# Loading v of two batches as fp32 through another queue, and turning x pair by pair, in a fused attention and squared-ReLU layer

## The chip, the cores and the metric

The kernel runs on one core of a Trainium2 chip. The metric is device time in microseconds (us), the median of the executions. The engines are TensorE (PE in the profile, PEld for its weight loads), VectorE (DVE), ScalarE (ACT), GpSimd (POOL) and SyncE (SP, which here issues transfers only). A line such as L1044 is line 1044 of the kernel before.

## The reference: what is computed

Attention with a relative bias over 8 batches of 8 heads, 576 positions and 64 dimensions, and then two dense layers with a squared ReLU between them:

```
B, H, S, D = q.shape                        # 8, 8, 576, 64, float32
scores = (1.0 / np.sqrt(D)) * np.matmul(q, k.transpose(0, 1, 3, 2))
scores = scores + bias.transpose(2, 0, 1)[None, :, :, :]   # bias_table[bucket(|i - j|)]
attn = np.exp(scores - max); attn = attn / (sum(attn) + 1e-09)
attn_out = np.matmul(attn, v)
x = attn_out.transpose(0, 2, 1, 3).reshape(B * S, H * D)   # 4608 x 512
h = np.maximum(x @ w_in, 0.0)               # w_in 512 x 2048
out = (h * h @ w_out)                       # w_out 2048 x 512, out float32
```

## The kernel before

The work on the chip is in fp16 with sums in fp32. A *pair* is two heads of one batch, so there are 32 pairs, four to a batch. A *group* is 512 rows of x, so there are nine; group 0 lies within batch 0. The program is laid out by a small planner at build time: each piece of work is added with the engines that may do it and their estimated durations, what it depends on, the buffers that it holds, a due time (its priority) and an earliest time; the planner then simulates all engines and writes the instructions in the order that it found. On the chip every engine runs its instructions in that order, each as soon as its data are there.

The constants that steer the plan (times in ns):

```
PERIOD, LEAD, FAST, FASTN = 9600.0, 1600.0, 3000, 7
AHEAD, G0, GP = 20600.0, 54700.0, 35900.0
RELU_DVE = 2
NSTG, NQK, NPT, NV, NX, NGB, NRT, NY = 5, 4, 3, 3, 6, 2, 4, 4
QUIET, LATER = 5200.0, 8500.0
TAB, EV = 6400.0, 1
ORDER = "k0 i0 q0 q1 v i1 i2 o0 k1 o1 i3 o2 o3"
...
def nominal(p):                       # when a pair is due
    return LEAD + FAST * min(p, FASTN) + PERIOD * max(p - FASTN, 0)
```

PSUM holds two score buffers of two banks, one bank for attention times v, and three banks (`g_ps`, ring `r_g`) for all else.

The first q and k come as fp32 into room of `g1` (a buffer that group 1 fills much later) and are cast. All other q, k, v and weights are loaded and cast to fp16 by transfers on GpSimd's queue. v of batch 0 goes head by head between the loads of q and k, v of batch 1 where ORDER has "v":

```
def load_v_head(b, h):
    l = load(
        "POOL", nc.gpsimd,
        lambda: vas[b_v[b].slot][:, :, h, 0:64],
        const(v[b, h, 0:512, :].rearrange("(t p) d -> p t d", p=128)),
        512 * 34.5, v_fix[min(b, 1)], [b_v[b]], pdue(),
    )
    ...
for hp in range(4):
    for w in range(2):
        if hp:
            load_six(hp, w)
        else:
            cast_first(w)
    if hp == 2:
        load_v_tail(0)
    if hp >= 1:
        for h in range(2 * hp - 2, 2 * hp):
            load_v_head(0, h)
for h in range(6, 8):
    load_v_head(0, h)
```

A few buffers have to be filled with constants once, by VectorE:

```
z_fix = [[fill(zz[:, 0], 0.0, 150.0, 10, QUIET)], [fill(zz[:, 1:], 0.0, 300.0, 11, LATER)]]
first = [fill(pt_sb[:, :, PW:], 1.0, 150.0, 20, LATER), fill(pm_sb[:, :, S:], 1.0, 150.0, 20, LATER)]
...   # v_fix: the same for the ones and zeros beside v
s_fix = [fill(stg[i][w][96:128, 512:640].bitcast(FP32), 0.0, 90.0, 40 + i, 25000.0) ...]
```

For the first three batches, q and k of a pair are turned by TensorE (L608) in twelve transposes each and evacuated by VectorE or ScalarE (L570, L572; pairs from 1 to EV-1 by VectorE alone):

```
if b < SIX:
    for j in range(6):
        for e in range(2):
            io(nc.tensor.transpose(ps[ds(64 * e, 64), ts(j, 96)], six(t)[:, e, ts(j, D)], id_sb[0:96, 0:96]))
```

A pair then goes on so: scores (L653, last queries L677, last keys L702), exponentials on ScalarE (L664, L687, L712), a multiply with the exponentials of the bias near the diagonal ("bands", VectorE, L745), attention times v with a column of sums (L781, L788), and a reciprocal and a multiply on VectorE (L805, L810), which leave x of the pair in SBUF. The bands need the bias tables, which TensorE builds (L353) and VectorE or ScalarE evacuates (L365, L367).

Layer 1 needs x turned. For batches 0 to 2 TensorE does this (L848) when all four pairs of the batch are through, one tile of 128 rows with four transposes at a time; for the later batches a transposing transfer does it:

```
def x_turn(b, norms):
    xb = [x_bufs[4 * b + hp] for hp in range(4)]
    for qt in range(5):
        bank = Buf(r_g)
        def tr(qt=qt, bank=bank):
            ps = g_ps[bank.slot].bitcast(FP16)
            for kk in range(4):
                io(nc.tensor.transpose(ps[:, ts(kk, 128)], xs[xb[kk].slot][:, qt, :], id_sb))
        ...
```

A tile of layer 1 is four matmuls over 512 columns (L1044), one for each pair of heads, as rows of x are 4 x 128 long. Its ReLU is done by ScalarE (L1065), or by either engine in groups below RELU_DVE (L1067), the square by VectorE (L1075). Layer 2 (L962) uses seven products of half matrices in place of eight.

```
def f1(nt=nt, bank=bank):
    ...
    for a, z, c in ((0, n, c), (n, GT, 0)):
        for kk in range(4 if z > a else 0):
            io(nc.tensor.matmul(g_ps[bank.slot][:, a:z], w_in_sb[:, kk, ts(nt, 128)],
                                xt_sb[:, kk, c : c + z - a], start=(kk == 0), stop=(kk == 3)))
...
o = P.add({"PE": 4 * mm(512)}, f1, xt_ready[g] + [l_win[nt // 4]], [bank, gb1], due + i * 2000, 0.0, "f")
```

Of the kernel before, what the change touches and what calls it, by code (L numbers as in the profile page):

```python
# [10 lines left out]
FP32 = mybir.dt.float32  # L11
# [19 lines left out]
PERIOD, LEAD, FAST, FASTN = 9600.0, 1600.0, 3000, 7  # L31
AHEAD, G0, GP = 20600.0, 54700.0, 35900.0
DT_X = 3
RELU_DVE = 2
NSTG, NQK, NPT, NV, NX, NGB, NRT, NY = 5, 4, 3, 3, 6, 2, 4, 4
QUIET, LATER = 5200.0, 8500.0
TAB, EV = 6400.0, 1
P_ORDER = "1 6 2 5 7 3 4"
P_LAST = "1 6 2 5 7 3 4"
SIX = 3  # L40
ORDER = "k0 i0 q0 q1 v i1 i2 o0 k1 o1 i3 o2 o3"
# [149 lines left out]
def kernel(  # L191
# [74 lines left out]
    def loader(eng_name, eng, out_, in_, packets, deps=(), bufs=(), due=0.0):  # L266
# [3 lines left out]
            {eng_name: 720.0 if eng_name == "POOL" else 600.0},  # L270
# [3 lines left out]
            due,  # L274
        )
# [10 lines left out]
    def load(eng_name, eng, out_, in_, packets, deps=(), bufs=(), due=0.0):  # L286
        return loader(eng_name, eng, out_, in_, packets, deps, bufs, due)[0]
# [15 lines left out]
        128 * 27, due=0,  # L303
# [21 lines left out]
        {"PE": 250.0},  # L325
# [21 lines left out]
    for c in range(6):  # L347
# [11 lines left out]
        o = P.add({"PE": 16 * 55.0}, t_mm, [o_eb, l_oh], [t_b], LEAD + TAB, 0.0, "f")  # L359
# [27 lines left out]
    def fill(ap, value, ns, due, after, deps=()):  # L387
# [3 lines left out]
    z_fix = [[fill(zz[:, 0], 0.0, 150.0, 10, QUIET)], [fill(zz[:, 1:], 0.0, 300.0, 11, LATER)]]  # L391
    first = [
        fill(pt_sb[:, :, PW:], 1.0, 150.0, 20, LATER),
        fill(pm_sb[:, :, S:], 1.0, 150.0, 20, LATER),
# [11 lines left out]
        fill(stg[i][w][96:128, 512:640].bitcast(FP32), 0.0, 90.0, 40 + i, 25000.0)  # L406
# [56 lines left out]
    def cast_first(w):  # L463

        def cast(o):
            src, dst = first_f[0:96, ts(w, 768)], stg[b_stg[0].slot][w][0:96, :]
# [6 lines left out]

    def load_v_head(b, h):
        l = load(
            "POOL", nc.gpsimd,
            lambda: vas[b_v[b].slot][:, :, h, 0:64],
            const(v[b, h, 0:512, :].rearrange("(t p) d -> p t d", p=128)),
            512 * 34.5, v_fix[min(b, 1)], [b_v[b]], pdue(),
        )  # L480
        l_v.setdefault((b, h // 2), []).append(l)
# [12 lines left out]
    def load_v(b):  # L494
# [9 lines left out]
        load_v_tail(b)  # L504

# [22 lines left out]
# [3 lines that stand above are left out]
                load_six(hp, w)  # L531
            else:
                cast_first(w)
        if hp == 2:
            load_v_tail(0)
        if hp >= 1:
            for h in range(2 * hp - 2, 2 * hp):
                load_v_head(0, h)
    for h in range(6, 8):
        load_v_head(0, h)  # L540
    for step in ORDER.split():
# [7 lines left out]
        else:  # L549
# [589 lines left out]
```

The softmax here doesn't subtract the row's maximum and nothing guards it: scores larger than these inputs give would overflow.

## Time and profile before

| | before |
|---|---|
| time, median of 3 | 377.01 us (376.7 to 378.59) |
| span of the profiled execution | 376.3 us |
| busy: TensorE, VectorE, ScalarE, GpSimd | 362.4, 269.0, 255.5, 178.3 us |
| transfers | 38.74 MB in 146,163 packets |
| software queue (GpSimd's) | 94,496 packets, 18.07 MB, 60.9% of the 16 engines |
| hardware queue (SyncE's) | 51,280 packets, 19.75 MB, 27.3% of the 16 engines |
| first matmul of L608 | 5.89 us |
| first matmul of layer 1 (L1044) | 41.24 us |

How to read it: the profile's page gives the busy time of each engine, the span cut into 40 slices with the busy share in tenths, the transfer queues, and the chain of work that ended last, followed back from the last instruction. A window gives the same busy times for one stretch. A busy TensorE isn't one at its peak, since matmuls overlap and their ends are modelled. Small groups of the page, in its columns (line, engine, operation, tiles, shapes and count; busy us and mean ns; idle time before them and what ended it), look so:

```profile
L271 POOL DMA_DIRECT2D va<-in_v_dram x36 | 30.8, 860 | 1.5 <-DMA qs<-in_q_dram 0.8
L635 POOL COPY qz<-kt 64x64 f16<-64x64 f16 x59 | 20.2, 342 | 33.3 <-DMA kt<-ks 17.4
```

The first is GpSimd issuing loads of v: 36 issues, 860 ns each. The second is a small copy on GpSimd.

### The profile page before, as it was taken

The numbers are of one execution on the slowest core, as the hardware profiler recorded it, in microseconds if no ns is written. First come the engines' busy times: TensorE is split into PE (matmuls) and PEld (weight loads), VectorE is DVE, ScalarE is ACT, GpSimd is POOL, SyncE is SP. The second block draws the span as 40 slices with busy tenths as digits, with TensorE's granted clock in tenths as the row PEclk, the third lists the DMA queues.
The fourth block names the chain that finished last, engine by engine and source line by source line (L and its number), as shares of the span: only waits on it lengthen the run. The fifth ranks groups of instructions, "written<-read, shape, count | busy, mean of one in ns | idle before, by whom it ended". The sixth has DMA issues, their size and how long they took to land.

```text
span 376.3 us, 10050 instructions
## 1 busy us (share of the span) xinstructions
PE 362.4 (96%) x4046; PEld 247.6 (66%) x4046; DVE 269.0 (71%) x612; ACT 255.5 (68%) x361; POOL 178.3 (47%) x318
## 2 busy tenths in 40 slices
PE   3988999999999999999999999999999999999996
PEld 2656555745778666687766765677577878556775
DVE  3987689998788677767685777757776683583653
ACT  4888979988557887866787778747885541564330
POOL 7876453889368583933758446583550000000000
PEclk9989999999999999999999999999999999999999
DMA  9999999699999999949999799999990222200103
GB/s 171 145 119 159 200 170 88 44 95 84 83 159 129 111 118 145 108 47 119 142 135 67 109 121 149 79 110 105 162 116 30 77 58 68 70 2 28 57 28 111
DMA packets 146163, 38.74 MB, mean 103 GB/s; under 512 B 128070, under 2 KB 146118, under 8 KB 146118
## 3 DMA queue, kind: packets, MB, share of 16 engines
q0 software_dynamic: 94496, 18.07, 60.9%
q1 hardware_dynamic: 51280, 19.75, 27.3%
q8 instruction: 31, 0.51, 0.6%
q10 hardware_dynamic: 342, 0.30, 0.3%
q14 instruction: 14, 0.11, 0.1%
HBM read 36.88 MB, written 9.44 MB: 123 GB/s over the span
## 4 chain that ended last, share of the span: by engine, by line
PE 90%; ACT 4%; DVE 3%; issue 1%; DMA 1%; ACTq 0%
PE f L1044 34%; PE f L962 29%; PE pv L788 10%; PE st L653 9%; PE pv L781 3%; PE st L702 2%; PE st L677 2%; ACT pt L664 1%; PE f L608 1%; DMA g<-in_k_dram 1%; ACT pt L687 1%; PE f L848 1%; DVE x L810 0%; ACT kt L570 0%; PE f L353 0%
## 5 line engine op out<-in xcount | busy, mean ns | idle before, releaser
L664 ACT ACTIVATE pt<-st 128x1024 f16<-128x1024 f32 x128 | 126.8, 1024 | 22.6 <-PE st L653 22.5
L1044 PE MATMUL f<-xt,w_in_sb 128*128 128x512 f16 (+4 forms) x704 | 142.1, 341 | 0.0
L1065 ACT ACTIVATE rt<-f 128x512 f16<-128x512 f32 x134 | 80.0, 598 | 62.0 <-PE f L1044 60.5
L1044 PEld LDWEIGHTS <-w_in_sb 128*128 128x128 f16 x704 | 62.6, 98 | 53.0 <-issue 10.8
L1075 DVE TENSOR_TENSOR g<-rt 128x512 f16<-128x512 f16 x144 | 60.7, 423 | 41.3 <-ACT rt L1065 40.2
L745 DVE TENSOR_TENSOR pt<-pt,tb_sb 128x1536 f16<-128x1536 f16 (+2 forms) x96 | 58.2, 621 | 10.6 <-ACT pt L664 10.2
L962 PEld LDWEIGHTS <-g 128*128 128x128 f16 x576 | 54.9, 98 | 15.4 <-issue 4.7
L788 PE MATMUL pv<-va,pt 128*128 128x65 f16 x1280 | 55.3, 194 | 0.0
L788 PEld LDWEIGHTS <-pt 128*128 128x128 f16 x1280 | 50.9, 98 | 2.9 <-issue 0.7
L271 POOL DMA_DIRECT2D qs<-in_q_dram x71 | 50.0, 725 | 2.4 <-DMA ks<-in_k_dram 1.1
L271 POOL DMA_DIRECT2D ks<-in_k_dram x71 | 50.0, 715 | 1.4 <-issue 1.4
L962 PEld LDWEIGHTS <-s 128*128 128x128 f16 x432 | 40.6, 98 | 10.6 <-issue 3.4
L635 POOL COPY qz<-qt 64x64 f16<-64x64 f16 x53 | 15.5, 293 | 64.2 <-DMA qt<-qs 35.5
L989 DVE SCALAR_TENSOR_TENSOR y<-f,y 128x512 f32<-128x512 f32 (+1 forms) x47 | 31.4, 667 | 16.1 <-PE f L962 15.1
L653 PE MATMUL st<-qt,kt 64*128 64x512 f16 x256 | 41.6, 396 | 1.1 <-ACT pt L664 0.5
L962 PE MATMUL f<-wt,g 128*128 128x256 f16 x288 | 36.6, 273 | 0.0
L962 PE MATMUL f<-w_out_sb,s 128*128 128x256 f16 x288 | 36.6, 273 | 0.0
L962 PE MATMUL f<-w_out_sb,g 128*128 128x256 f16 x288 | 36.2, 273 | 0.1
L781 PE MATMUL pv<-vm,pm 128*128 128x130 f16 x160 | 35.5, 222 | 0.5 <-DVE x L810 0.4
L635 POOL COPY qz<-kt 64x64 f16<-64x64 f16 x59 | 20.2, 342 | 33.3 <-DMA kt<-ks 17.4
L810 DVE TENSOR_TENSOR x<-pv,r 128x384 f16<-128x384 f32 x64 | 31.4, 490 | 1.9
L271 POOL DMA_DIRECT2D va<-in_v_dram x36 | 30.8, 860 | 1.5 <-DMA qs<-in_q_dram 0.8
(62 smaller groups left out, 308.0 us busy)
## 6 DMA issues: line engine op xcount, KB each, us to landing
out_dram<-y SPq DMA_DIRECT2D x34, 256.0 KB, 2.4
va<-in_v_dram POOLq DMA_DIRECT2D x28, 128.0 KB, 4.7
qs<-in_q_dram POOLq DMA_DIRECT2D x40, 64.0 KB, 3.2
ks<-in_k_dram POOLq DMA_DIRECT2D x40, 64.0 KB, 3.0
w_in_sb<-in_moe_w_in_dram POOLq DMA_DIRECT2D x4, 512.0 KB, 7.6
w_out_sb<-in_moe_w_out_dram POOLq DMA_DIRECT2D x4, 512.0 KB, 9.9
qs<-in_q_dram POOLq DMA_DIRECT2D x11, 144.0 KB, 5.0
ks<-in_k_dram POOLq DMA_DIRECT2D x11, 144.0 KB, 6.2
```

The source lines that it names most:

```text
L271: lambda: io(eng.dma_start(out=out_(), in_=in_())),
L635: io(eng.tensor_copy(out=dst[qb.slot][rw, rw], in_=src[qb.slot][rw, 512:576]))
L653: nc.tensor.matmul(sets_ps[st.slot][:, e, :], kt[rw, ts(jt, 128)], qt[rw, 0:512], start=True, stop=True,)
L664: nc.scalar.activation(out=p5(pts[pb.slot])[:, jt, :, 0:512], in_=sets_ps[st.slot], func=EXPF, scale=SCALE)
L745: io(nc.vector.tensor_tensor(out=a, in0=a, in1=t, op=MULT))
L781: nc.tensor.matmul(ps[:, i, :, :], pm[:, c : c + 128], vm[:, hp, :, 0:65], start=True, stop=False)
L788: nc.tensor.matmul(ps[:, i, e, :], pt[:, (2 * jt + e) * S + c : (2 * jt + e) * S + c + 128], va[:, jt, 2 * hp + e, 0:65], start=False, sto ...
L810: nc.vector.tensor_tensor(out=xs[xb.slot][:, qt0 : qt0 + nq, :].rearrange("p t (e d) -> p t e d", e=2), in0=ps[:, :, :, 0:64], in1=rs[rb.s ...
L962: nc.tensor.matmul(g_ps[bf.slot][:, ts(s_, HALF)], left(c, s_), right(c), start=(c == 0 and (s_ == 0 or apart) and i not in before), stop= ...
L1044: nc.tensor.matmul(g_ps[bank.slot][:, a:z], w_in_sb[:, kk, ts(nt, 128)], xt_sb[:, kk, c : c + z - a], start=(kk == 0), stop=(kk == 3),)
L1065: io(nc.scalar.activation(out=rts[rb.slot], in_=g_ps[bank.slot], func=RELUF))
L1075: nc.vector.tensor_tensor(out=gs[gb1.slot][:, nt, :], in0=rts[rb.slot], in1=rts[rb.slot], op=MULT)
```

## The change

It has three parts that can be seen in the data flow. v of batches 0 and 1 is fetched as fp32 through SyncE's queue into the upper part of `g1`, which group 1 needs only later, and cast by GpSimd into place; that takes these loads, with their cast, off GpSimd's queue. x is turned by pairs, not by batches, so that a pair's x is ready for layer 1 as soon as the pair is through. The first three tiles of layer 1 (PRE) are split: three of the four matmuls run when three pairs are there, the fourth when all are. Beside these, pair 0 is turned by six transposes of both heads at once, for which its cast lays the heads side by side; VectorE alone evacuates q and k of pairs 1 to 6 (EV); the constant fills come earlier (QUIET, LATER, FILL); the planner's estimates of several operations are set anew; the order of loads and the due times are others. The option PV_G is off.

The diff, cut to its core:

```
-PERIOD, LEAD, FAST, FASTN = 9600.0, 1600.0, 3000, 7
-AHEAD, G0, GP = 20600.0, 54700.0, 35900.0
+PERIOD, LEAD, FAST, FASTN = 8800.0, 2300.0, 3100.0, 8
+AHEAD, G0, GP = 22400.0, 56700.0, 44600.0
-RELU_DVE = 2
+RELU_DVE = 3
-QUIET, LATER = 5200.0, 8500.0
-TAB, EV = 6400.0, 1
-P_ORDER = "1 6 2 5 7 3 4"
+QUIET, LATER = 1500.0, 1500.0
+TAB, EV = 9000.0, 7
+P_ORDER = "1 2 6 5 7 3 4"
-ORDER = "k0 i0 q0 q1 v i1 i2 o0 k1 o1 i3 o2 o3"
+PV_G, PRE, FILL = 0, 3, 0
+V0_AT, V1_AT = 4600.0, 25300.0
+ORDER = "k0 i0 q0 k1 q1 i1 i2 i3 o0 o1 o2 o3"
...
-        o = P.add({"PE": 16 * 55.0}, t_mm, [o_eb, l_oh], [t_b], LEAD + TAB, 0.0, "f")
+        o = P.add({"PE": 16 * 33.0}, t_mm, [o_eb, l_oh], [t_b], LEAD + TAB, 0.0, "f")
...   (fills: 150 to 170 and 220, 300 to 380 ns)
-        fill(stg[i][w][96:128, 512:640].bitcast(FP32), 0.0, 90.0, 40 + i, 25000.0)
+        fill(stg[i][w][96:128, 512:640].bitcast(FP32), 0.0, 90.0, 40 + i, FILL)
...
+    room_f = gs[NGB - 1].bitcast(FP32).rearrange("p t c -> p (t c)")[:, 1536:]
+    def fetch_v(b):
+        rb = Buf(r_room)
+        for tt in range(4):
+            l = load("SP", nc.sync,
+                const(room_f[:, ts(tt, 512)].rearrange("p (h d) -> p h d", h=H)),
+                const(v[b, :, ts(tt, 128), :].transpose([1, 0, 2])),
+                1024 * 19, (), [rb], -0.5 + b, after=(V0_AT, V1_AT)[b])
+            o = P.add({"POOL": 780.0},
+                lambda tt=tt: io(nc.gpsimd.tensor_copy(
+                        out=vas[b_v[b].slot][:, tt, :, 0:64],
+                        in_=room_f[:, ts(tt, 512)].rearrange("p (h d) -> p h d", h=H))),
+                [l] + v_fix[min(b, 1)], [rb, b_v[b]], -1.0)
...   (the last 64 rows likewise: two loads and two casts of 420 ns)
-        if hp == 2:
-            load_v_tail(0)
-        if hp >= 1:
-            for h in range(2 * hp - 2, 2 * hp):
-                load_v_head(0, h)
-    for h in range(6, 8):
-        load_v_head(0, h)
+    for b in range(2):
+        fetch_v(b)
...
+                if p == 0:
+                    for j in range(6):
+                        io(nc.tensor.transpose(ps[:, ts(j, 96)], t[0:96, ts(j, 128)], id_sb[0:96, 0:96]))
...
-    def x_turn(b, norms):
+    def x_turn(p, norms):
+        b, hp = divmod(p, 4)
+        for part, qt0, nq in ((0, 0, 3), (1, 3, 2)):
+            bank = Buf(r_g)
+            n = min(128 * nq, S - 128 * qt0)
+            def tr(qt0=qt0, nq=nq, bank=bank):
+                ps = g_ps[bank.slot].bitcast(FP16)
+                for i in range(nq):
+                    io(nc.tensor.transpose(ps[:, ts(i, 128)], xs[xb.slot][:, qt0 + i, :], id_sb))
+            o = P.add({"PE": nq * mm(128)}, tr, [norms[part]], [bank, xb], T, 0.0, "f")
...   (one copy of 384 or 192 columns each, and xt_pair notes it)
+                ahead = 3 if g == 0 and i < PRE else 0
+                if ahead:
+                    o = P.add({"PE": ahead * mm(512)}, lambda f1=f1: f1(k1=3),
+                        [x for kk in range(ahead) for x in xt_pair[g, kk]] + [l_win[nt // 4]], [bank, gb1],
+                        due + i * 2000, 0.0, "f")
                 o = P.add(
-                    {"PE": 4 * mm(512)}, f1, xt_ready[g] + [l_win[nt // 4]], [bank, gb1], due + i * 2000, 0.0, "f"
+                    {"PE": (4 - ahead) * mm(512)}, lambda f1=f1, ahead=ahead: f1(k0=ahead),
+                    [o] + (v_cast if g == NGB - 1 else []) + xt_ready[g] + [l_win[nt // 4]], [bank, gb1], ...
```

## The prediction

> **What bounds the kernel now.** I read the page first, for who is busy, then the chain of waits, then windows of the first 80 us, then the timelines of the engines in the first 42 us. The page says TensorE (PE):
>
> ```profile
> PE 362.4 (96%) x4046; PEld 247.6 (66%) x4046; DVE 269.0 (71%) x612; ACT 255.5 (68%) x361; POOL 178.3 (47%) x318
> ...
> PEclk9989999999999999999999999999999999999999
> DMA  9999999699999999949999799999990222200103
> ...
> PE 90%; ACT 4%; DVE 3%; issue 1%; DMA 1%; ACTq 0%
> ```
>
> The Trainium skill ("Trainium Kernel Development and Optimization", Performance Expectations) warns that matmul busy time flatters, since matmuls overlap, and this trace agrees: the page's 96% hides gaps. So I add up what TensorE streams, with lengths read off the chain where it runs without a break: four layer-1 matmuls 0.86 us, 144 tiles: 124; eight layer-2 matmuls 0.87 us, 126 times: 110; a query tile of attention times v 0.06 + 0.24 us, 160 times: 48; four score matmuls 0.43 us, 64 times: 27.5; last keys 0.24 and last queries 0.22 us, 32 times each: 14.7; twelve transposes of q or k 0.315 us, 24 times: 7.6; x turned and bias tables about 6.5. Sum 338 us of a span of 376.3. The other 38 us: 5.9 before the first matmul, about 3 after the last, and 29 in gaps that busy time does not show. Layer 1 starts at 41.2 us. By then the trace has 40 score matmuls, 20 query tiles, 168 transposes of q and k, 96 table matmuls, 12 + 24 of the last keys and queries and 20 of x: 4.3 + 6.0 + 4.4 + 3.2 + 2.7 + 1.1 = 21.7 us of streaming in 35.3 us. So some 13.6 us are lost there and some 16 us in the 332 us after. The latter are mostly a fixed toll: a layer-1 tile after a change of the array's row mode takes 0.97 us instead of 0.86, and 54 groups of four scores lie after 41 us, each with a change in and out: 54 x 2 x 0.11 = 11.9 us. The change leaves those groups as they are. What can be won lies before 41 us.
>
> What limits that stretch is seen in the windows (columns: length, then busy us of PE, its weight loads, VectorE, ScalarE, GpSimd, granted clock, DMA share, GB/s):
>
> ```profile
> 14.00:18.00 4.00, 4.00 (x82) 2.67 (x78) 3.83 (x9) 3.50 (x5) 3.58 (x6) 1.00 1.72 111
> 18.00:22.00 4.00, 2.87 (x32) 1.52 (x33) 3.79 (x9) 3.79 (x6) 3.64 (x7) 0.84 1.11 147
> 22.00:26.00 4.00, 3.99 (x75) 3.00 (x73) 2.91 (x8) 3.21 (x6) 1.89 (x5) 0.73 1.78 137
> 26.00:30.00 4.00, 3.69 (x89) 2.95 (x89) 3.52 (x18) 4.00 (x6) 3.60 (x8) 1.00 0.89 58
> ```
>
> VectorE and ScalarE are both nearly full; TensorE waits for exponentials and for evacuated q and k. The clock dips there. The chain of waits in this stretch (start, length, what) shows whose work it is:
>
> ```profile
> 5.89 1.19 PE f L608 x24
> ...
> 8.97 0.38 DVE qz L388
> 9.35 0.21 DVE pt L388
> 9.56 0.21 DVE pm L388
> ...
> 9.83 0.50 DVE vm L388
> ...
> 10.63 0.77 DVE kt L572
> ...
> 24.80 1.03 ACT kt L570 x2
> 25.82 1.70 ACT pt L664 x2
> ...
> 40.32 0.45 PE f L848 x5
> 40.77 0.54 PE st L653 x4
> 41.31 2.70 PE f L1044 x12
> ```
>
> From 9 to 10.6 us the chain is nothing but memsets on VectorE (two short ones of 0.14 and 0.07 us follow those shown); at 24.8 it is ScalarE evacuating k ahead of exponentials. v is not on it: its eight head loads for batch 0 are issued from 7.5 to 16.6 us and land a median 4.7 us later, and the first attention times v, at 21.75 us, follows band multiplies on VectorE that begin at 20.28.
>
> **What the skill says.** "SBUF — State Buffer", SBUF: two separate sides: GpSimd and VectorE share one port pair, held for a whole instruction; it names VectorE operations in a two-port mode or with two SBUF inputs, and says that a GpSimd-queue DMA is held up when its descriptors can't be written. This trace is compatible: the same GpSimd copy of 64x64 takes 0.23 us alone, and four from 51.43 us took 2.47. "GPSIMD Engine Reference", Elementwise: a one-input loop at 1.8 cycles an element, 512 elements in 769 ns; no run here shows a fp32 cast on GpSimd yet. "DMA: Bandwidth & Descriptors", Why small descriptors are slow: a fixed overhead per packet, 27% for one of 256 B. The page of the profile agrees in kind: 94,496 software packets hold 60.9% of 16 engines, 376.3 x 16 x 0.609 / 94,496 = 38.8 ns each, though most are small.
>
> **The change, part by part.**
> 1. Memsets. Their earliest planned times go from 5.2 and 8.5 us to 1.5 us, where VectorE is idle (0.83 to 5.28 us), and the ten of the staging rows (26.20 to 26.97 us) to the start. On the chain this removes 0.38 + 0.21 + 0.21 + 0.50 + 0.14 + 0.07 = 1.5 us, and off it some 1.5 us of a nearly full VectorE. Gain 1.5 us.
> 2. Pair 0's q and k are turned by 6 transposes each instead of 12, as the cast lays both heads side by side: 24 took 1.19 us in the chain, 12 should take 0.6. Gain 0.6 us.
> 3. q and k of pairs 1 to 6 are evacuated by VectorE alone. ScalarE did 4 qt and 3 kt before 41.2 us (2.7 + 1.8 us), all but one of pairs after 0, so it loses about 3.9 us; VectorE gains six of 0.75, 4.5 us, less the 3.2 us of memsets taken away. The least work before batch 0 is through: ScalarE from 8.8 us, 4 pairs of 4 x 1.02 + 0.65 + 0.60 = 5.3 us, 21.3, and four or five further pieces of batch 1; VectorE from 5.9 us, tables 4.4, evacuations of pairs 0 to 5 about 8.3, bands 4 x (0.42 + 0.95 + 0.48 + 0.25) = 8.4, normalising 4 x (0.20 + 0.56 + 0.18 + 0.42) = 5.4, x 2.3, small copies 1.6: 30.4 us, so 36 us without a wait. VectorE now is the limit; ScalarE's relief is worth perhaps 1.5 us, not 3.9.
> 4. x turned pair by pair. The last norm of batch 0 ends at 40.27 us, layer 1 starts 1.0 us later; now only one group of two transposes and a copy of 192 columns stand between, about 0.7 us. Twenty transposes stay twenty, but eight copies replace five in each of three batches: 9 x about 0.2 us more on VectorE or ScalarE. About nothing.
> 5. First three tiles with three of four pairs: 9 matmuls of 0.216 us, 1.9 us, move into gaps before batch 0 is through. At least one of three banks must stay free for turning x, so I count 1.2 us.
> 6. v of batches 0 and 1. GpSimd loses 12 + 4 issues, 12 x about 0.75 + 4 x 0.63 = 11.5 us, and gets 8 casts of 128x512 and 4 small ones: with 0.77 us and half of it, 7.7 us. GpSimd is not the bound. On the DMA engines 2 x 4,608 software packets go, at the 38.8 ns mean 22 us of all sixteen, and as many fp32 ones of 256 B come, at the 32.0 ns mean of the hardware queue (376.3 x 16 x 0.273 / 51,280) 18 us, perhaps less. Since v was not on the chain, that is worth nothing by itself. It costs: SyncE has no wait ahead of these loads, so it will issue them right behind its third load (1.68 us), earlier than planned, and they share the engines with k of pair 0, which lands at 5.26 us and ends the first wait, and pairs 1 to 3. I take 0.7 us. The casts meet VectorE's two-input band multiplies at the shared port: 12 casts, a third of them in the way for half a length, 12/3 x 0.4 = 1.6 us on a full VectorE, half on the chain, 0.8.
> 7. New periods, priorities and VectorE relus in group 2: they only reorder. I put 0.
>
> Sum: 1.5 + 0.6 + 1.5 + 1.2 - 0.7 - 0.8 = 3.3 us, and a bit for the clock dip, which fewer gaps would shorten: 0.9. Layer 1 then starts at about 37 us, and since TensorE goes on unbroken the end moves with the work done by then: 377.0 - 4.2 = 372.8 us.
>
> **Rivals.** *The start is only a loan*: if layer 1 starts earlier but batch 1 is less far, ScalarE (full from 62 to 80 us, for example 3.92 of 4 us busy at 62 to 66) makes TensorE wait later, and the time stays at 376 to 377. Against it: TensorE has 16 tiles of layer 1 and all of layer 2 of group 0 (26 us) to fill with. *v becomes the bound*: late landing on a crowded queue, or GpSimd standing in order at a cast while loads of q and k wait behind it, puts 3 to 6 us on the first attention times v: 377 to 381. For it speaks the DMA share of 9 throughout the first 20 slices but one; against it that v is needed only at 21 us. *The whole 13.6 us at the start shrink by more than half* because the order planned now fits the chip's real durations (the new estimates are the trace's: 16 table matmuls at 33 ns, memsets of 0.22 and 0.38 us): 369 or below. VectorE's 36 us speak against it.
>
> **Range and chances.** The gains of the start are bounded by 13.6 us, of which VectorE's work keeps more than half; two costs could eat all of them. So 368 to 378 us holds eight in ten. 2% is 7.5 us, a time under 369.5: it needs the third rival, 0.16. Over 384.5 needs a new wait of 8 us or more that repeats, 0.05. Within: 0.79.
>
> **What would show it.** Layer 1's first matmuls at about 37 us, partial ones earlier; no memset after 6 us; pair 0's transposes half as many; ScalarE without evacuations of pairs 1 to 6, VectorE over 3.7 of 4 us busy from 10 to 34; v casts of 0.8 us, longer where bands run; k of pair 0 landing at 5.3 to 6 us; gaps after 41 us unchanged. I am wrong if casts of v or their loads end waits of TensorE, if layer 1 starts later than 39 us, or if it starts near 37 and the end does not follow.

## The result, and the profile after

| | before | after |
|---|---|---|
| time, median of 4 each | 377.29 us (376.7 to 378.59) | 382.03 us (381.97 to 382.59) |
| ratio, 95% interval | | 1.0124 (1.0095 to 1.0153) |
| span of the profiled execution | 376.3 us | 379.9 us |
| first attention times v | 21.75 us | 23.0 us |
| layer 1: first matmul, first whole tile | 41.24 us | 43.25 us (three quarters of a tile), 46.4 us |

The change makes the kernel slower by 1.2%, which is little, but the whole interval lies above 1. In after, lines have moved: L1088 is layer 1 (before L1044), L1006 layer 2, L699, L723 and L748 the scores, L827 and L834 attention times v, L612 VectorE's evacuation of q and k, L681 the small copies of last keys and queries, L518 and L542 the new casts of v.

The page of after, in the lines that were shown of before:

```profile
PE 361.5 (95%) x4034; PEld 247.8 (65%) x4034; DVE 274.2 (72%) x618; ACT 251.2 (66%) x358; POOL 174.5 (46%) x320
...
PEclk9959999999999999999999999999999999999999
DMA  8999991499999999959999699898990230010103
...
PE 86%; DVE 6%; DMA 5%; ACT 1%; issue 1%; SPq 0%; POOL 0%; ACTq 0%
```

One slice of the clock, the third, has gone from 8 to 5, and transfers hold 5% of the chain instead of 1%. The windows of the same stretch (columns as before: length, then busy us of PE, its weight loads, VectorE, ScalarE, GpSimd, granted clock, DMA share, GB/s) show where:

```profile
14.00:18.00 4.00, 1.54 (x28) 0.90 (x27) 3.93 (x9) 2.98 (x5) 0.34 (x1) 1.00 1.23 194
18.00:22.00 4.00, 1.28 (x14) 0.74 (x15) 0.06 (x1) 0.65 (x1) 1.53 (x4) 0.50 0.96 201
22.00:26.00 4.00, 2.96 (x39) 2.04 (x40) 1.00 (x4) 0.58 (x1) 3.90 (x9) 0.50 1.22 225
26.00:30.00 4.00, 3.64 (x66) 2.89 (x61) 2.44 (x5) 2.86 (x5) 2.18 (x5) 0.72 1.30 197
```

Before, TensorE was busy for 2.87 to 4.00 of each 4 us here. Now TensorE, VectorE and ScalarE stand for most of the time from 18 to 22 us, and the clock is at 0.50 from 18.0 to 28.3 us (before, from 20.8 to 24.2), so that eight matmuls of attention times v take 0.44 us at first instead of 0.24. Transfers ran at 194 to 225 GB/s all the time. The chain of waits says for what (start, length, what):

```profile
7.16 14.37 DMA g<-in_v_dram
...
21.58 0.61 POOL va L518
...
22.59 0.41 POOL vm L542
...
23.04 0.27 PE pv L827
```

The whole way to the first attention times v is the transfer of v of batch 0, then the last casts. GpSimd's timeline (start, length, engine, line, operation, tiles, count, and in brackets its idle time before and what ended it) adds the second half:

```profile
17.66 0.61 POOL L518 CAST va<-g 128x512 f16<-128x512 f32 x1 [5.89 <-DMA g<-in_v_dram]
18.33 0.23 POOL L681 COPY qz<-kt 64x64 f16<-64x64 f16 x1
20.49 0.61 POOL L518 CAST va<-g 128x512 f16<-128x512 f32 x1 [1.93 <-DMA g<-in_v_dram]
```

GpSimd stood 5.9 us at the second cast, and behind it, in order, waited a copy of last keys. The waits of the stretch from 5 to 46.4 us (engine, tile, line, what it waited for: us in total, times, longest) name both:

```profile
PE pv L827 <- POOL vm L542: 3.1, 1, 3.1
...
PE st L748 <- POOL qz L681: 2.7, 1, 2.7
```

TensorE stood from 15.97 to 18.6 us for that copy and from 19.9 to 23.0 us for v.

For comparing runs I use one more measure, as the prediction did for the time up to 41.2 us: at a moment t, t less the streaming time of all matmuls begun by then (lengths at full clock; 338 us in all). That is what TensorE has lost by t:

| lost by (us) | 22 | 30 | 38 | 50 | 70 | 100 |
|---|---|---|---|---|---|---|
| before | 13.6 | 15.8 | 18.9 | 20.4 | 22.1 | 24.3 |
| after | 15.2 | 19.5 | 21.7 | 23.7 | 26.2 | 28.6 |
| e5, v of batch 0 in large packets | 11.6 | 13.8 | 15.2 | 16.3 | 19.5 | 21.0 |
| e1, v of both on GpSimd's queue | 12.2 | 13.8 | 16.0 | 17.3 | 21.4 | 23.1 |
| e16, v of batch 1 held | 13.9 | 16.0 | 18.3 | 19.3 | 22.4 | 24.1 |
| e17, and two copies first | 11.7 | 13.8 | 15.1 | 21.3 | 24.4 | 26.5 |
| e18, and held less long | 11.2 | 13.5 | 14.9 | 19.3 | 22.3 | 24.1 |

After has lost 4.3 us more than before by 100 us, and 3.8 us more at 320 us (37.6 against 33.8). Of that, 3.7 us are there by 30 us: most of the damage is done early.

### The profile page after: what moved, and what is told of

The parts are those of the page before. It is cut to its first block, busy times and chain, and to the rows that moved or that the text cites. A ratio compares the mean times of both kernels' runs of the same rounds, so it can differ in the third digit from the quotient of the medians.

```text
span 379.9 us, 10063 instructions
## 1 busy us (share of the span) xinstructions
PE 361.5 (95%) x4034; PEld 247.8 (65%) x4034; DVE 274.2 (72%) x618; ACT 251.2 (66%) x358; POOL 174.5 (46%) x320
## 4 chain that ended last, share of the span: by engine, by line
PE 86%; DVE 6%; DMA 5%; ACT 1%; issue 1%; SPq 0%; POOL 0%; ACTq 0%
PE f L1088 33%; PE f L1006 29%; PE pv L834 9%; PE st L699 8%; DMA g<-in_v_dram 4%; PE pv L827 3%; PE st L748 2%; PE st L723 2%; DVE pt L791 1%; DMA g<-in_k_dram 1%; DVE s L965 1%; DVE kt L612 1%; DVE x L856 1%; PE f L897 1%; DVE qt L612 1%; PE f L651 1%
## 5 line engine op out<-in xcount | busy, mean ns | idle before, releaser
L1088 PE MATMUL f<-xt,w_in_sb 128*128 128x512 f16 (+4 forms) x704 | 143.3, 341 | 0.1
L710 ACT ACTIVATE pt<-st 128x1024 f16<-128x1024 f32 x128 | 126.0, 1024 | 26.0 <-PE st L699 25.9
L1118 ACT ACTIVATE rt<-f 128x512 f16<-128x512 f32 x127 | 75.8, 598 | 67.4 <-PE f L1088 65.0
L1088 PEld LDWEIGHTS <-w_in_sb 128*128 128x128 f16 x704 | 62.7, 98 | 47.9 <-issue 8.1
L1006 PEld LDWEIGHTS <-g 128*128 128x128 f16 x576 | 54.8, 98 | 15.5 <-issue 4.7
L791 DVE TENSOR_TENSOR pt<-pt,tb_sb 128x512 f16<-128x512 f16 (+2 forms) x96 | 58.9, 632 | 7.6 <-ACT pt L710 7.1
L834 PE MATMUL pv<-va,pt 128*128 128x65 f16 x1280 | 55.8, 195 | 0.0
L834 PEld LDWEIGHTS <-pt 128*128 128x128 f16 x1280 | 51.4, 98 | 5.3 <-issue 3.4
L681 POOL COPY qz<-qt 64x64 f16<-64x64 f16 x62 | 19.8, 320 | 65.7 <-DMA qt<-qs 29.3
L1006 PEld LDWEIGHTS <-s 128*128 128x128 f16 x432 | 40.4, 98 | 12.2 <-issue 4.2
L699 PE MATMUL st<-qt,kt 64*128 64x512 f16 x256 | 40.7, 389 | 1.0 <-ACT pt L733 0.6
L1033 DVE SCALAR_TENSOR_TENSOR y<-f,y 128x512 f32<-128x512 f32 (+1 forms) x47 | 31.3, 666 | 11.2 <-PE f L1006 10.5
L827 PE MATMUL pv<-vm,pm 128*128 128x130 f16 x160 | 35.7, 223 | 3.3 <-POOL vm L542 3.1
L1006 PE MATMUL f<-wt,g 128*128 128x256 f16 x288 | 36.7, 273 | 0.0
L1006 PE MATMUL f<-w_out_sb,s 128*128 128x256 f16 x288 | 36.7, 273 | 0.0
L1006 PE MATMUL f<-w_out_sb,g 128*128 128x256 f16 x288 | 35.9, 273 | 0.0
L681 POOL COPY qz<-kt 64x64 f16<-64x64 f16 x56 | 16.9, 302 | 26.5 <-DMA kt<-ks 23.7
L965 DVE TENSOR_TENSOR s<-g,s 128x1024 f16<-128x1024 f16 x36 | 24.8, 689 | 0.4
```

The source lines that it names most:

```text
L681: io(eng.tensor_copy(out=dst[qb.slot][rw, rw], in_=src[qb.slot][rw, 512:576]))
L699: nc.tensor.matmul(sets_ps[st.slot][:, e, :], kt[rw, ts(jt, 128)], qt[rw, 0:512], start=True, stop=True,)
L710: nc.scalar.activation(out=p5(pts[pb.slot])[:, jt, :, 0:512], in_=sets_ps[st.slot], func=EXPF, scale=SCALE)
L791: io(nc.vector.tensor_tensor(out=a, in0=a, in1=t, op=MULT))
L827: nc.tensor.matmul(ps[:, i, :, :], pm[:, c : c + 128], vm[:, hp, :, 0:65], start=True, stop=False)
L834: nc.tensor.matmul(ps[:, i, e, :], pt[:, (2 * jt + e) * S + c : (2 * jt + e) * S + c + 128], va[:, jt, 2 * hp + e, 0:65], start=False, sto ...
```

## The experiments

Each time is a median; the ratio is to runs of the kernel before on the same chip (377.0 to 377.6 us), with its 95% interval.

### Is it v's packets? e5, e1, e7

Why should 1.2 MB take from 2.2 to 21.6 us when 200 GB/s flow? Theory A: v comes in packets of 256 bytes, and the transfer engines take packets from the queues in turn, so v gets a small part of the bytes beside packets of 768 and 1,024 bytes on GpSimd's queue. In e5 the same number of bytes goes to the same places with the same issues, but is read from consecutive addresses, in runs of 1 and 2 KB. It takes the values of v of batch 0 from wrong places, so it computes something else; its time shows what the packets cost.

```
-  const(v[b, :, ts(tt, 128), :].transpose([1, 0, 2]))          # 64 floats a piece
+  const(flat_v_of_batch[65536 * tt : 65536 * (tt + 1)].rearrange("(p h d) -> p h d", p=128, h=H) if b == 0 else ...)
   (the last 64 rows likewise)
```

> The changed kernel with the six loads of v of batch 0 reading the same number of bytes as runs of 2 KB (1 KB for the last rows) in place of 256 B; the values land in wrong places, so it computes something else; every engine's order of instructions is the same. If the number of packets holds v back (each takes its turn with one larger packet of GpSimd's queue): the last cast of v of batch 0 ends at 12 to 15 us in place of 23.0, the first attention times v at 16 to 19 us, 377 to 378.5 us. If the bytes alone do (all engines moved about 200 GB/s until 24 us): the last cast still ends after 19 us and 380 us or more.

Measured: 373.53 us, ratio 0.9903 (0.9866 to 0.9939). The casts of batch 0 run from 10.7 to 14.7 us, the first attention times v at 17.3, partial tiles of layer 1 at 35.3 us. That is 3.5 us less than even the better of the two expectations had it. Its windows:

```profile
14.00:18.00 4.00, 3.40 (x75) 2.47 (x72) 3.94 (x10) 4.00 (x6) 3.12 (x6) 1.00 1.24 197
18.00:22.00 4.00, 3.65 (x79) 2.50 (x76) 3.93 (x10) 3.26 (x5) 3.45 (x6) 1.00 1.29 210
```

VectorE is full, the clock is 1.00, and the bytes per second are what they were; from 6 to 14 us, where v now comes through, they are more (254 and 255 GB/s against 193). With the same order on every engine, the packets of batch 0's v cost 382.03 - 373.53 = 8.5 us. The rest of the change, with v on time in this way, is worth 3.8 us or so, near the 4.2 that the prediction had for all of it.

In before the same rows of v went as 4,608 packets of 128 bytes between 5 and 20 us, but in GpSimd's own queue, in order with the loads of q and k. There was no second full queue to take turns with.

e1 leaves the rest of the change as it is and puts v of both batches back on GpSimd's queue (v of batch 0 between the loads of q and k, batch 1's after q of batch 1). The planner then finds another order.

```
-    for b in range(2):
-        fetch_v(b)
+   ... load_v_tail(0), load_v_head(0, h) between the pairs, as in before
-ORDER = "k0 i0 q0 k1 q1 i1 i2 i3 o0 o1 o2 o3"
+ORDER = "k0 i0 q0 k1 q1 v i1 i2 i3 o0 o1 o2 o3"
```

> The changed kernel with v of batches 0 and 1 back on GpSimd's queue, cast by the transfer, as before; all else as changed, the plan made anew. Theory A (v lands late: v's 256-byte packets take turns with packets of 768 and 1024 bytes, so v of batch 0 is complete at 22 us in the changed kernel and TensorE stands from 15.9 to 23): the first attention times v at 17 to 19 us, no TensorE clock of 0.50, 372 to 375 us. Theory B (VectorE alone is the cause: it evacuates q and k of pairs 1 to 6 and is full from 29 to 46 us): 379 to 382 us, layer 1 still after 44 us.

Measured: 377.47 us, ratio 1.0004 (0.9987 to 1.0021). First attention times v at 18.1, layer 1 at 37.8 us, as the prediction had it, and yet the time is that of before, between what theories A and B said. The gain of 3.1 us at 50 us (17.3 against 20.4) is 0.7 at 70. The chain of waits of e1 in that stretch:

```profile
57.95 0.69 DVE rt L1136
...
59.34 0.70 DVE s L981
60.07 0.70 DVE s L981
...
62.09 2.01 DVE pt L807 x4
```

Group 0's sixteen tiles of layer 1 are used up at 57.9 us, and then VectorE has its last ReLU, the sums of activations for layer 2 (s) and four band multiplies of batch 1 one after the other, while TensorE has little. So the start was a loan here: the rival that the prediction called so. (The order is another than in after, so e1 alone doesn't tell what the place of v is worth.)

e7 is the other way round: before with the new v and nothing else.

```
 (before)  - load_v_head, load_v_tail, load_v(1)      + fetch_v(0), fetch_v(1)
```

> The kernel before with v of batches 0 and 1 fetched as fp32 on SyncE's queue and cast by GpSimd, and nothing else of the change. Theory A: v of batch 0 complete at 19 to 22 us, where the kernel before needs it at 21.75 and gives GpSimd copies that stand behind the casts: 378 to 381 us. If v's cost in the changed kernel comes only with its other parts: 376.5 to 378.

Measured: 386.24 us, ratio 1.0238 (1.0197 to 1.028), worse than either theory had it. The casts of 128x512 take 0.61 to 1.33 us in it, and the first attention times v comes at 24.0. So the part with v costs 8.7 us alone, in an order that the planner made anew for it, and the rest of the change gives back 4.2.

### What crowds v out, and does GpSimd's order matter? e2, e3, e4

e2 puts w_in's first quarter (packets of 1,024 bytes) behind q and k of batch 1; every other engine keeps its order.

```
-ORDER = "k0 i0 q0 k1 q1 i1 i2 i3 o0 o1 o2 o3"
+ORDER = "k0 q0 k1 q1 i0 i1 i2 i3 o0 o1 o2 o3"
```

> The changed kernel with the first quarter of w_in issued behind the loads of q and k of batch 1 in place of ahead of them; the order of instructions on TensorE, VectorE, ScalarE and SyncE is the same. Theory A: 1 MB less in v's way, the last cast of v of batch 0 ends at 18 to 20 us instead of 23.0, 378 to 380 us. Theory B: 381.5 to 382.5 us.

Measured: 379.88 us, ratio 1.0063 (1.004 to 1.0086); first attention times v at 20.9 us, 2.1 sooner than after, and the time 2.15 us less.

e3 holds all loads of GpSimd's queue that come after pairs 1 to 3 behind the last cast of batch 0.

```
+   held = GpSimd's issues between pair 3's q and k and the last cast of batch 0
+   ... the last cast, held, ...
```

> The changed kernel with all loads on GpSimd's queue after those of pairs 1 to 3 issued behind the last cast of v of batch 0; the order on all other engines is the same. Theory A: v of batch 0 has only pairs 1 to 3 beside it, its last cast ends at 14 to 16 us, TensorE no longer stands before 23 us, 375 to 378 us, unless the loads of pairs 4 and 5 now come too late (then pairs 4 and 5 are turned late and it stays at 380). Theory B: 381.5 to 382.5 us.

Measured: 380.02 us, ratio 1.0068 (1.0046 to 1.0089); first attention times v at 18.7 us, but now TensorE's weight loads wait for k of pairs 4 and 5 (3.0 us in two waits). Whoever is put behind pays: the transfers of this stretch ran at some 200 GB/s here too (155 to 250, by windows of 2 us from 10 to 30 us).

e4 asks whether it is only GpSimd's order, and puts the copy of last keys that waited ahead of the second cast.

```
-   ... cast va (second), copy qz<-kt ...
+   ... copy qz<-kt, cast va (second) ...
```

> The changed kernel with one exchange in GpSimd's order: the small copy of k of pair 1, which the last keys of pair 1 wait for until 18.6 us, ahead of the second cast of v. Theory A in its narrow form (the landing of v itself sets the time): last keys run at about 16 us but the first attention times v stays at 23.0 us, 381 to 382 us. Theory C (it is standing in order behind a cast that costs): 379 to 380 us.

Measured: 382.08 us, ratio 1.0113 (1.0096 to 1.013). The wait for the copy is gone, and the wait of attention times v for the last cast has grown from 3.1 to 6.2 us instead:

```profile
PE pv L827 <- POOL vm L542: 6.2, 1, 6.2
```

In after it is the landing of v that counts; the order hides behind it.

### Other suspects: e8, e6

Theory B was that VectorE, which alone evacuates q and k of pairs 1 to 6, is overloaded. e8 is e1 with both engines again (and two split tiles, since the planner finds no order with three):

```
-TAB, EV = 9000.0, 7      PRE = 3
+TAB, EV = 9000.0, 1      PRE = 2
```

> The changed kernel with v on GpSimd's queue (as in the first experiment, 377.5 us) and q and k of pairs 1 to 6 evacuated by either engine again; PRE is 2, as the plan doesn't come out with 3. Theory B (VectorE alone evacuating them is what keeps the gain away): 374 to 376 us. Theory L: 376.5 to 378 us, with layer 1 starting at 37 to 40.

Measured: 378.44 us, ratio 1.0023 (1.001 to 1.0036), no less than e1 (1.0 us more, at the edge of what the intervals tell apart). Theory B falls, and e5 speaks against it too: VectorE has the same evacuations there, is full, and the time is 373.5 us.

e6 is before with the earlier fills alone:

```
-QUIET, LATER = 5200.0, 8500.0     ... fill(stg...,  25000.0)
+QUIET, LATER = 1500.0, 1500.0     ... fill(stg...,  0.0)
```

> The kernel before with the constant fills planned from 1.5 us, and those of the staging rows from 0, and nothing else of the change. Prediction's step 1 with its end carried over unbroken: 375.5 to 376. Theory L (what is won before layer 1 is a loan, since TensorE runs out of layer 1 of group 0 before batch 1 is through): layer 1 starts 1 to 1.5 us earlier and the time is 376.5 to 377.5.

Measured: 379.84 us, ratio 1.0068 (1.0047 to 1.0088): slower, which neither had. Layer 1 begins 0.6 us sooner, but the new order puts sums of weights, between evacuations of q, k and x, on VectorE in the chain from 70.8 to 78.1 us, and group 1's layer 1 begins at 78.2 instead of 75.6 us. A new order of the planner can thus cost some 2 us, which is why the last four runs keep it.

### Can layer 2 fill the hole, and is batch 1's v harmless? e9, e10, e11, e14

e9 is e1 with the sums of weights due earlier, so that layer 2 could be used as filler:

```
-                    l + [o], (), 1e5,
+                    l + [o], (), 30000.0,
```

> The kernel with v of both batches back on GpSimd's queue, in which layer 1 began at 37.8 us but the time was 377.5, now with the eight sums of weights that VectorE makes for layer 2 due at 30 us in the plan instead of 100 us, so that layer 2 of group 0 may be used as filler earlier. Theory L (the early start was lost again because between 58 and 70 us TensorE ran out of tiles that it may do, as layer 2's products wait for those sums): the loss at 58 to 70 us shrinks and the time is 374 to 376. Theory B2 (VectorE's evacuations for batch 1 and ScalarE's exponentials limit that stretch whatever TensorE may fill with): the loss stays and the time is 377 to 378.5.

Measured: 379.28 us, ratio 1.0049 (1.003 to 1.0067). Theory L, in the form that layer 2 waits for the sums of weights, falls: the loss from 58 to 66 us is 3.1 us, against 3.0 in e1. What held TensorE there was the sums of activations and the bands on VectorE, not the sums of weights. That e9 takes 1.8 us more than e1 comes mostly after 70 us (0.4 of it is there by then), and its cause stays open.

e10 has v of batch 0 on GpSimd's queue and v of batch 1 through SyncE's; e11 is the same with the earlier sums.

```
-    for b in range(2):
-        fetch_v(b)
+    ... load_v_tail(0), load_v_head(0, h) between the pairs; fetch_v(1)
```

> After, but only v of batch 1 as fp32 through SyncE's queue; v of batch 0 head by head on GpSimd's queue as before. Theory A (the harm is v of batch 0 alone, whose small packets must come through in the first 22 us beside the larger ones of q, k and w_in; v of batch 1 has until about 50 us): first attention times v at 18 to 19 us, layer 1 at 37 to 38.5, time 374 to 377. Rival (v of batch 1 on SyncE's queue costs as well, as the loads issued behind it come late): over 378.

> The same, v of batch 0 on GpSimd's queue and v of batch 1 through SyncE's, and the sums of weights due at 30 us. If both of my readings hold, this is the best of the three that compute the whole: 373 to 375.5, under before by 0.4 to 1%. If VectorE limits the stretch from 45 to 75 us, the sums done early only take its time from evacuations, and it is no better than without: within 0.5 us of that kernel or slower.

Measured: e10 382.36 us (the median with one execution of 923.95 us in it, 382.28 without), ratio 1.0117 (1.0095 to 1.0139), e11 381.54 us, 1.0114 (1.0058 to 1.017). But SyncE's timeline of e10 shows that this told nothing of the question:

```profile
2.15 12.21 SPq L273 DMA_DIRECT2D g<-in_v_dram  x6
```

The room was free, so nothing on the chip held batch 1's v: it went out at 2.15 us, into the same crowd, and k came late. An earliest time in the plan is no wait. e14 was to hold it by a dependence on pair 3's q and k:

```
-                1024 * 19, (), [rb], -0.5 + b, ...
+                1024 * 19, l_qk[3, 0] + l_qk[3, 1], [rb], -0.5 + b, ...
```

> v of batch 0 on GpSimd's queue as before, v of batch 1 as fp32 through SyncE's queue, held until q and k of pair 3 have landed. If only the crowd of the first 15 us harms: layer 1 at 37.5 to 38.5 us, time 376 to 378, as with v of both batches on GpSimd's queue (377.5). If 4,608 small packets harm wherever they stand, since q, k and weights behind them come late: over 379.

Measured: 382.33 us, ratio 1.0136 (1.0079 to 1.0194), and SyncE again issued at 2.15 us; that dependence, too, ordered only the plan. So e14 is e10 once more: with 4,608 small packets first that nobody needs before 45 us the time is 5 us over that of e1. The traces show 1.1 us (e10) and 2.7 us (e14) of that lost by 50 us; the rest came later, and as both have an order of their own, it is not shown that the packets cost it.

### Two queues for the small packets? e12, e13

If each queue has its turn, two queues of small packets should have two. e12 lets ScalarE issue two of the four large loads at 2.7 us, where it is idle; e13 also puts w_in late.

```
-                "SP", nc.sync,
+                "SP", nc.scalar if b == 0 and tt % 2 else nc.sync,     # and moved to the front of ScalarE's order
```

> After, with two of the four large loads of v of batch 0 (the second and the fourth) issued by ScalarE at 2.7 us, where it is idle, in place of SyncE; every engine's order is otherwise the same and v still goes in packets of 256 bytes. Theory A, by queue (each queue gets its turn, so two queues of small packets get two turns for one of GpSimd's queue): the four casts are through by about 16 us instead of 22, first attention times v at 18 to 20 us, layer 1's partial tiles at 38 to 40, time 376 to 379. Rival (the two queues share one turn, or the engines are simply full, and q and k then land as much later): first attention times v at 22 to 24, time 381 to 383.

> The same with w_in's first quarter behind q and k of batch 1 on GpSimd's queue. If both help by what they take out of the same stretch (w_in late alone gave 379.9): first attention times v at 17 to 19 us, time 374.5 to 377. If q and k of pairs 1 to 3 then come late instead, as when those loads were held: 378 to 380.

Measured: e12 382.68 us, ratio 1.0148 (1.0117 to 1.0179), e13 380.8 us, 1.0097 (1.0069 to 1.0124): nothing gained over after and e2. The packets counted in the traces say why (number and mean ns by queue and size; B is bytes):

```
             GpSimd's 768 and 1,024 B   SyncE's 256 B    ScalarE's 256 B
after   5-10 us    689                  1447, 22.6 ns          -
       10-14       572 + 144             725, 30.1             -
       14-18       279 + 368             656, 30.8             -
       18-22       105                  2788, 18.7             -
e12     5-10       643                  1019, 21.5          534, 24.2
       10-14       573 +  51             610, 30.0          662, 19.2
       14-18       115 + 428             544, 30.9          558, 18.5
       18-22       307 +  33            2034, 20.5          294, 18.7
e17    30-34         0 + 606             612, 30.9             -
```

While two queues are full, they pass equal numbers of packets (656 to 647, 612 to 606), whatever their size, and so do three (543, 544, 558). It is not SyncE's issuing that held v back in after: once GpSimd's queue was nearly empty, from 18 us, 2,788 small packets went in 4 us.

So the share rose as theory A says: from 5 to 18 us 3,927 small packets went in e12, against 2,828. But the last load of batch 0 was not there sooner (last casts at 21.7 and 22.3 us), and the reason is the rival's: what v gained, q, k and w_in lost. From 5 to 18 us GpSimd's queue passed 1,810 packets in e12 and 2,052 in after, so in e12 it was still busy when in after it had almost ended. From 18 to 20 us it passed 153 and 125 in a us, and the last 294 of ScalarE's queue went beside them at 147 and 111, until 20.9 us. SyncE, once its part was done, went on to batch 1's v, about 1,650 packets of which ran before 22 us. With batch 1's v held, e12 was not tried.

The Trainium skill ("DMA: Bandwidth & Descriptors", Queues, rings and completion order) says that each transfer engine goes round its queues packet by packet, a packet there being typically 9 to 17 descriptors. The trace agrees with the turns; in what the profile counts as packets the numbers are equal, and how many go in one turn can't be read from them. The same page (Issuing engines are not separate DMA queues) says that more issuing engines save only the issuing; for the time of e12 that holds (382.68 us against 382.03), for the share of the packets it does not.

### The same order with v elsewhere: e15, e16, e17, e18

The last four keep the order of after on TensorE, VectorE and ScalarE and move only loads of v and small work on GpSimd. In e15 GpSimd loads v of both batches, batch 0's behind q and k of pair 3, batch 1's where after casts it. In e16 only batch 0's; batch 1's goes through SyncE as in after, held by a fill of one column of its room on GpSimd.

```
 e15  - SyncE's loads and the casts        + nc.gpsimd.dma_start(out=vas[...], in_=v[b, :, ts(n, 128), :]...)
 e16  as e15 for b = 0; for b = 1          + nc.gpsimd.memset(room_f[:, 0:1], 0.0)   # SyncE's first load of batch 1 waits for it
```

> After with the loads of v of batches 0 and 1 issued by GpSimd into place, cast by the transfer as before, and every other engine in exactly the order of after: batch 0's six loads behind pair 3's q and k, batch 1's where after casts it. Theory O (the missing gain with v on GpSimd's queue was the re-planned order of the other engines): v of batch 0 lands by 15 to 17 us, first attention times v at 17.5 to 19, partial tiles of layer 1 at 35.5 to 37.5 us, time 373.5 to 375.5, under before. Theory Q (v on GpSimd's queue takes from q, k and weights what they need, whatever the order): layer 1 as early, but time 376.5 to 378.5.

> The same for batch 0; v of batch 1 as fp32 through SyncE's queue with casts on GpSimd as in after, its first load held by a fill of one column of the room on GpSimd behind the third load after batch 0's copies, about 20 to 24 us. If small packets harm only where they meet what is needed first: within 1 us of the run before it (373.5 to 376). If they harm wherever they stand: over by 2 us or more.

Measured: e15 381.13 us, ratio 1.0091 (1.0057 to 1.0126); e16 377.24 us, 0.999 (0.9978 to 1.0002). In e15 batch 1's v stands in GpSimd's queue behind w_out and lands at 50.7 us, and TensorE waits:

```profile
PE pv L827 <- DMA vm<-in_v_dram: 2.5, 1, 2.5
```

With its own queue (e16) it does not, and that is worth 3.9 us, which is the purpose of the change. But this holds against loads that stand where after has its casts; e1, whose GpSimd issues them sooner, takes 377.47 us, as e16 does. Early on e16 was held back elsewhere (its timeline and waits from 6 to 20 us):

```profile
13.12 0.23 POOL L681 COPY qz<-kt 64x64 f16<-64x64 f16 x1
```

```profile
PE st L748 <- POOL qz L681: 2.4, 1, 2.4
```

Six issues of v, of 0.66 to 0.95 us each, and three of k and w_in stand ahead of a copy of 0.23 us. e17 moves two such copies ahead of the issues of v's last rows, of k and of w_in, and nothing else:

```
-   va x4, vm x2, k, w_in, k, copy, q, copy, copy ...
+   va x4, copy, copy, vm x2, k, w_in, k, q, copy ...
```

> The run with v of batch 0 on GpSimd's queue and v of batch 1 held on SyncE's, with two of GpSimd's 64x64 copies put ahead of the issues of v's last rows, of k of pairs 4 and 5 and of w_in's first quarter; all else in the same order. If the wait of TensorE for that copy was what this run lacked: last keys of pair 0 at about 10.7 us instead of 13.4, first attention times v at 18 to 19 instead of 20.6, time 373.5 to 375.5, under before by 0.5 to 1%. If v in GpSimd's queue is late itself: first attention times v stays at 20 us or later, time 376.5 to 377.5.

Measured: 380.24 us, ratio 1.0078 (1.0058 to 1.0098), outside both expectations. Up to 38 us it is e5 again (15.1 us lost against 15.2; attention times v at 17.4 against 17.3). Then, in its timeline and waits:

```profile
41.50 0.61 POOL L518 CAST va<-g 128x512 f16<-128x512 f32 x1 [5.88 <-DMA g<-in_v_dram]
42.06 0.53 POOL L681 COPY qz<-qt 64x64 f16<-64x64 f16 x2
```

```profile
PE st L723 <- POOL qz L681: 4.1, 1, 4.1
```

It is the fault of after a second time, with batch 1's v: GpSimd stands at a cast, and TensorE at a copy behind it. SyncE issued batch 1's v from 17.6 us, and its packets came one for one beside w_in and w_out, 612 in 4 us, which is 30 us for all 4,608. TensorE is now early, and they are late: this cast waits until 41.5 us, where in e16 it ran at 36.9. e18 frees them sooner, at 14 us:

```
-   ... k (17.5 us), fill, q ...
+   ... q (14.0 us), fill, copy, copy, q, k, k ...
```

> The last kernel with the fill that holds v of batch 1 moved forward on GpSimd, from behind k of pair 5's successor (17.5 us) to behind the last load of pair 4 and 5 that precedes the copies (about 14.4 us). While both queues are full, 612 small and 606 large packets went in each 4 us, one for one, so 3 us more are some 500 to 1,100 packets of the 4,608, and the third cast should come 4 to 7 us sooner, at 34.5 to 37.5 us instead of 41.5. If that wait took the gain: TensorE's 4 us wait at 38 us goes, last cast at 44 to 47 us, time 373.5 to 376. If the earlier start only slows batch 0's q, k and w_in instead: first attention times v after 18.5 us or a new wait before 38 us, time 377 to 380.

Measured: 378.29 us, ratio 1.003 (1.0012 to 1.0048). The third cast comes 3.2 us sooner, where 4 to 7 were expected, the wait for the copy shrinks to 1.6 us, but the last cast is at 48.5 us, and the waits from 36 to 56 us say:

```profile
PE pv L827 <- POOL vm L542: 2.2, 1, 2.2
```

Batch 1's v now sets the end of its own first attention. The direction was right and the size short. No kernel that computes the whole came out under before by more than the measurement tells (e16: 0.999).

## Why the prediction was wrong

The time lies above the range (368 to 378). By the steps of the prediction:

- **Steps 1 to 5 in sum, and "the end moves with it": held in e5, where v is on time.** e5 gives 373.5 us against 372.8, its first whole tile of layer 1 comes at 38.5 us, and the clock is at 1.00. But e5 computes something else; of the kernels that compute the whole, with the same steps, none got under 377.2 us. The single terms are less sure. Step 2 failed: pair 0's twelve transposes took 1.1 us (from 5.99 to 7.1), as long as the 24 before (1.19): each turns twice as much, and its time is no shorter in sum. The 0.6 us was nothing. Step 1's memsets all ended by 4.4 us, but alone (e6) they brought layer 1 forward by 0.6 us, not 1.5. Step 3's 1.5 us: undone in e8, with one split tile fewer and another order, the time rose by 1.0 us, which is hardly clear of noise. Steps 4 and 5 were not tried alone.
- **Step 6 failed, and it is 8.5 of the 9.2 us of the miss.** It added up engine time (18 us of sixteen engines for v of both batches) and took 0.7 us off for sharing, and said "since v was not on the chain, that is worth nothing by itself". It measured 8.5 us for batch 0 alone (after against e5). The engine time was not even short: 256-byte packets took 18.7 ns when alone and 30.9 beside others, near the 32.0 assumed. What was missing is that a queue of small packets gets one turn for each large packet of the other queue: 4,608 packets at some 150 in a us are 30 us if the other queue stays full, and even with that queue's pauses v landed only at 21.6 us, with casts still to come. That v was not on the chain before told only that the old loads were early enough. The 0.8 us for casts at the shared port was generous: in after seven of the eight large ones took 0.61 us, one 0.87 (in e7 up to 1.33).
- **The clock** went the other way: it went to 0.50 at 18.0 us, while TensorE stood, and stayed there for 10.2 us; in e5, without that gap, it was at 1.00. I had counted on 0.9 us of gain. What sets it is not shown: in e16 a gap of 2.4 us left it at 1.00.
- **Rival "v becomes the bound"** named both halves, the late landing and GpSimd standing in order at a cast, with 377 to 381 us for it. It was the right one, and still too small by 1 us. The argument I put against it, that v is needed only at 21 us, was the wrong one: I did not ask when it could be there, and the change itself moves the need forward (17.3 us in e5).
- **Rival "a loan"** is what happens in e1: with layer 1 at 37.8 us the time stays at 377.5. I had argued that TensorE has 16 tiles and all of layer 2 to fill with; the tiles were gone at 58 us, and layer 2 has to wait for VectorE's sums of activations.

What stays open: where e10's executions, from 379.2 to 383.9 us, differ, since its profile is of the shortest; and what a planner that knew the real landing of v would make of the 3.7 us between e16 and e5.

## What to carry to other kernels

Count the packets of a transfer, not its bytes: here small ones went one for one beside a full queue of large packets (612 to 606 in 4 us), so 4,608 of 256 bytes would take some 30 us however little they weigh, and a transfer that leaves the chain free today can become the chain when it is moved to another queue. An earliest time or a dependence that only the plan knows held nothing (e10 and e14 issued at 2.15 us); a fill that the load had to wait for did (e16, 21.0 us). On an engine that works in order, look at what stands behind a step that waits for a transfer: here a copy of 0.23 us stopped TensorE for 2.4 to 4.1 us.

## What the runs showed that I had not expected

- Full queues passed packets one for one: two of them (606 of 1,024 bytes, 612 of 256 in 4 us of e17) and three (543, 544, 558 in e12). A 256-byte packet took 18.7 ns alone and 30.9 ns beside 1,024-byte ones, which took 96.3.
- SyncE stood long at some issues: in after its first two loads of v took 0.46 and 0.58 us to issue, the next three 1.75, 6.25 and 4.54 us; in e5, in large packets, batch 0's six took 0.33 to 0.73 us. That its queue had no more room is my reading and not shown.
- Twelve transposes of 96x128, both heads at once, took as long as 24 of 96x64: 1.1 to 1.2 us.
- A cast of 128x512 from fp32 to fp16 on GpSimd took 0.61 us in most places.
